# Rows of four q loads moved between DMA engines, in a kernel of sliding-window attention and spectral mixing on one core

## The chip, the core and the metric

The kernel runs on one core of a Trainium2 chip. The metric is the device time of one execution in microseconds (us). Before the change three runs gave 424.06, 424.40 and 424.67 us, median 424.4. The profiled execution took 424.43 us; its span, from the first to the last instruction, is 422.7 us.

## The reference, cut to what matters

```python
# q, k, v: (8, 8, 576, 64) float32; w_r, w_i: (64, 512, 512); w_ch: (512, 512)
scores = q @ k^T / 8, kept where 0 <= i - j < 64, softmax over j
x = (softmax @ v), the 8 heads side by side            # (8, 576, 512)
X = rfft(x, over the 576 positions)[:, :64]            # 64 modes
Yr = Xr w_r - Xi w_i ; Yi = Xr w_i + Xi w_r            # a 512x512 matrix pair for each mode
u = x + irfft(Y)
out = u + max(u @ w_ch, 0)
```

The 64 pairs of mode weights are 134 MB in float32 and are each used once. They are most of what the kernel reads: with q, k, v and `w_ch` it is 162.53 MB by the page's own account.

## The kernel before

The work goes in three stages. In the first (to about 142 us) eight batches of attention run, each with its rows of q, k and v loaded as bfloat16 (the transfer casts), turned on TensorE and used in windows of 512 score columns; the transform to 64 modes follows each batch. In the second (to about 389 us) the 127 weight matrices that are used are multiplied one after the other as they arrive; between them TensorE does the channel product and the inverse transform of what is complete. In the third the last rows are finished and written out.

All large loads are issued by GpSimd (POOL) in one order, and pass through the core's 16 DMA engines. `load` (line 117) loads one batch of q, k or v into a tile of 128 partitions with two runs of 2,304 bytes each; `load_w` (152) loads one mode's matrix, 4,096 bytes for each of 128 partitions, and `load_two` (157) loads two. A transfer over 128 partitions gives each DMA engine eight partitions: a q load is 16 packets of 2,304 bytes on each engine, a matrix 8 packets of 4,096.

The order in the first stage is written by hand. Unit 2, 5 and 8 of batch b's turning work frees the raw tile of k, v or q, and `refill` (422) then loads the same input of batch b + 2 and, if b > 0, one more early weight. So the requests go k, weight, v, weight, q, weight, batch after batch. The q loads of batches 4, 5, 6 and 7 are issued at 45.24, 58.27, 75.94 and 88.97 us. Eight DMA semaphores serve POOL's transfers in turn, so that each request also waits until the transfer eight before it has landed on all engines.

One load is uneven already (111 to 125): the q of batch 7. Its first 128 rows (the lower four heads) are split. 125 rows go as a transfer whose source is seen as 5 blocks of 25 rows with the block index outermost in the walk, so that 5 DMA engines carry 25 rows each and 11 carry none; the last 3 rows go by themselves; and a small transfer `aside` of 22 rows of 32 bytes in 11 blocks carries no data that is used. The code takes it that transfers on fewer than 16 engines get their engines in turn, and `aside` completes the turn: 5 and 11 engines. The upper 128 rows go evenly. As the 125 rows then lie in another order in the tile, the transposes of these rows use `back` (115, 262 to 264) instead of the identity: a permuted identity that two VectorE copies make from `ident_bf`.

`part` (258) turns six columns of a raw tile on TensorE into `pst`, and `evac` (55) copies them out.

Of the kernel before, what the change touches and what calls it, by code (L numbers as in the profile page):

```python
# [11 lines left out]
BF16 = mybir.dt.bfloat16  # L12
# [8 lines left out]
def view(ap, off, dims):  # L21

    return bass.AP(ap.tensor, ap.offset + off, [list(ap.ap[0])] + [list(d) for d in dims])
# [3 lines left out]
def kernel(  # L27
# [10 lines left out]
    nc = tc.nc  # L38
    B, H, S, D = q.shape
# [8 lines left out]
    RUN = S // 32  # L48
# [6 lines left out]
    def evac(o, i, on_act):  # L55

        if on_act:
            return nc.scalar.copy(out=o, in_=i)  # L58
        return nc.vector.tensor_copy(out=o, in_=i)  # L59
# [10 lines left out]
    ident_bf = consts.tile([128, 128], BF16, name="ident_bf")  # L70
# [19 lines left out]
    acons = p1.enter_context(tc.tile_pool(name="acons", bufs=1, side="right"))  # L90
# [12 lines left out]
    def raw_tile(which):  # L103
        return rawp.tile([128, 2, RUN * D], BF16, name="r" + which)

    def runs(b, which):
        return RAW[which][b].rearrange("(x g) (p c) d -> (g p) x (c d)", g=4, c=RUN)

    UNEVEN = (B - 1, "q")
    FEW, MORE = 5, 25
    LOT = FEW * MORE
    aside = acons.tile([2 * (16 - FEW), 16], BF16, name="aside")
    back = acons.tile([128, 128], BF16, name="back")

    def load(b, which):
        r = raw_tile(which)
        if (b, which) == UNEVEN:
            lower, upper = [RAW[which][b, x * H // 2:(x + 1) * H // 2].rearrange("g (p c) d -> (g p) (c d)", c=RUN)  # L120
                            for x in range(2)]
            nc.gpsimd.dma_start(out=r[:LOT, 0, :], in_=lower[:LOT].rearrange("(r a) c -> a r c", a=FEW))
            nc.gpsimd.dma_start(out=r[:, 1, :], in_=upper)
            nc.gpsimd.dma_start(out=r[LOT:, 0, :], in_=lower[LOT:])
            nc.gpsimd.dma_start(out=aside, in_=lower[:2 * (16 - FEW), 0:16].rearrange("(r a) c -> a r c", a=16 - FEW))
        else:
            nc.gpsimd.dma_start(out=r, in_=runs(b, which))
        raws[b, which] = r
# [65 lines left out]
    with tc.manual_schedule(engines=ALL_FOUR):  # L194
# [3 lines left out]
        with tc.tile_pool(name="tmpf", bufs=1, side="right") as tmp:  # L198
            mo = tmp.tile([128, NM], FP32, name="mo")
            to = tmp.tile([128, NT], FP32, name="to")  # L200
            nc.gpsimd.iota(mo, pattern=[[1, NM]], base=0, channel_multiplier=0,
                           allow_small_or_imprecise_dtypes=True)
            nc.gpsimd.iota(to, pattern=[[128, NT]], base=0, channel_multiplier=1,
                           allow_small_or_imprecise_dtypes=True)
            nc.gpsimd.memset(ident, 0.0)
            nc.gpsimd.affine_select(out=ident, in_=ident, compare_op=ALU.not_equal, fill=1.0,
                                    base=0, pattern=[[-1, 128]], channel_multiplier=1)
            load(0, "q")
            load(0, "v")
            for t0, t1 in ((0, 3), (3, NT)):  # L210
                n = t1 - t0
                mt = tmp.tile([128, 2, n * NM], FP32, name="mtf")
                nc.vector.tensor_tensor(out=view(mt, 0, [[NM, n], [1, NM]]), in0=view(mo, 0, [[0, n], [1, NM]]),
                                        in1=view(to, t0, [[1, n], [0, NM]]), op=ALU.mult)
                gen_trig(tmp, mt, n * NM, trigF[:, t0:t1, 0:NM], trigF[:, t0:t1, NM:2 * NM], "f")
                if t0 == 0:
                    nc.vector.tensor_copy(out=ident_bf, in_=ident)
        nc.scalar.activation(out=spark, in_=ident[:, 0:1], func=ACT_F.Exp)
        raws[0, "k"] = raw_tile("k")
        for c, engine in enumerate((nc.vector, nc.gpsimd, nc.vector)):  # L220
            cc = slice(6 * D * c, 6 * D * (c + 1))
            engine.tensor_copy(out=raws[0, "k"][:, :, cc], in_=k_first[:, :, cc])
        load(1, "k")
        for i in range(4):
            half = i % 2
# [24 lines left out]
    def transpose_units(b):  # L250

        rk, rq, rv = (raws.pop((b, which)) for which in "kqv")
        qT = qtp.tile([128, 4, S], BF16, name="qT")
        vT = vtp.tile([128, 4, S], BF16, name="vT")
        kT, vt = kTs[b % 2], vts[b % 2]
        qTs[b] = qT

        def part(src, dst, c0, on_act, uneven=False):
            def f():
                ps = ps_misc.tile([128, 6, 128], BF16, name="pst", tag="misc")  # L260
                if uneven and c0 == 0:
                    nc.vector.tensor_copy(out=back, in_=ident_bf)
                    nc.vector.tensor_copy(out=view(back, 0, [[1, FEW], [FEW, MORE]]),
                                          in_=view(ident_bf, 0, [[MORE, FEW], [1, MORE]]))
                for c in range(6):
                    for hh in range(2):
                        nc.tensor.transpose(out=ps[64 * hh:64 * hh + 64, c, :],  # L267
                                            in_=src[:, hh, (c0 + c) * D:(c0 + c + 1) * D],
                                            identity=back if uneven and hh == 0 else ident_bf)
                evac(view(dst, c0, [[S, 4], [RUN, 32], [1, 6]]),  # L270
                     view(ps, 0, [[32, 4], [1, 32], [128, 6]]), on_act)
            return f

        def vback(u):
            def f():
                ps = ps_misc.tile([128, 6, 128], BF16, name="psv", tag="misc")
                for i in range(6):
                    a, j = divmod(6 * u + i, 9)
                    if j == 4:
                        parts = [(0, 64, 2 * a, 512), (64, 64, 2 * a + 1, 0)]  # L280
                    else:
                        parts = [(0, 128, 2 * a + (j > 4), 128 * j - (j > 4) * S)]
                    for r0, n, g, t0 in parts:
                        nc.tensor.transpose(out=ps[r0:r0 + n, i, :],  # L284
                                            in_=vT[:, g, t0:t0 + n], identity=ident_bf)
                evac(view(vt, 6 * u * VW, [[18 * VW, 2], [VW, 6], [1, D]]),
                     view(ps, 0, [[D, 2], [128, 6], [1, D]]), u != 1)
                if u:
                    hs = slice(u - 1, u + 2, 2)
                    nc.vector.tensor_copy(out=vt[64:128, 1, hs, 1:9], in_=vt[64:128, 0, hs, 0:8])  # L290
                    nc.vector.tensor_copy(out=vt[0:64, 1, hs], in_=vt[0:64, 0, hs])
            return f

        return [part(rk, kT, 0, True), part(rk, kT, 6, False), part(rk, kT, 12, True),
                part(rv, vT, 0, False), part(rv, vT, 6, True), part(rv, vT, 12, False),
                *(part(rq, qT, 6 * i, i != 1, (b, "q") == UNEVEN) for i in range(3)),
                vback(0), vback(1), vback(2)]

    def head_of(n):
# [48 lines left out]
    def closes(w):  # L348

        return min(-(-8 * w // 9) * 9 or 9, 8 * w + 8)  # L350
# [92 lines left out]
    with tc.manual_schedule(engines=ALL_FOUR):  # L443
        first = transpose_units(0)
        for j in (0, 1, 2, 6, 7, 8):
            first[j]()
            refill(0, j)
            if j in (2, 8):
                warm_up(3)
        for half in range(2):  # L450
            pp = slice(64 * half, 64 * half + 64)
            nc.vector.tensor_copy(out=band2[pp], in_=band[pp, half, :])
        mask(0, 1)
        scores(0)
        for j in (3, 4, 5):
            first[j]()
            refill(0, j)
            warm_up(2)
        for vt in vts:
            nc.vector.memset(vt[:, 0, :, :, 64:66], 1.0)  # L460
        for j in (9, 10, 11):
            first[j]()
            refill(0, j)
        nc.vector.memset(pso, 1.0)
        nc.vector.tensor_copy(out=ident_r, in_=ident)
    with tc.manual_schedule(engines={E.PE, E.Pool}):
# [9 lines left out]
        def unit(b, j):  # L476
            if b not in units:
                units[b] = transpose_units(b)
            units[b][j]()
            refill(b, j)  # L480
            turned(b, j)

        for w in range(NWIN + 1):
# [5 lines left out]
            n = len(todo)  # L489
            if 0 < w < NWIN:  # L490
                scores(w)
            if w:
                cut = closes(w - 1)
# [12 lines left out]
            if w in (NWIN - 4, NWIN - 1):  # L506
                i = (B - 2) % 2 if w == NWIN - 4 else (B - 1) % 2
                spare(kTs[i])
                spare(qtp.tile([128, 4, S], BF16, name="qT"))
            if w in (NWIN - 4, NWIN):  # L510
                i = (B - 2) % 2 if w == NWIN - 4 else (B - 1) % 2
# [386 lines left out]
    for k, (f, delta, n, few) in enumerate(items):  # L898
        i = S_I + k * (T_I - 2 - S_I) // len(items)
# [25 lines left out]
    with tc.manual_schedule(engines=ALL_FOUR):  # L925
# [92 lines left out]
        for k in range(6):  # L1018
# [10 lines left out]
                              in_=view(psys[0], 0, [[2 * B, NC], [2, B], [1, 2]]))  # L1029
# [78 lines left out]
```

## Time and profile before

| what | value |
|---|---|
| time of the profiled execution, its span | 424.43 us, 422.7 us |
| median of three runs | 424.4 us |
| first stage, attention | 0 to 142 us |
| weights still to catch up with | 142 to 176 us |
| weights as they land | 176 to 389 us |
| last weight landed, on all engines | 389.20 us |
| from there to the end of the span | 33.5 us |
| transfers issued by POOL | 126 |

The page counts the busy time of each engine, shows the span in 40 slices, the DMA queues, and the chain of work that ended last. The chain is read from the last instruction back: each step is what released the one after it. The list of DMA issues gives each transfer's size and the time from issue to its last landing. Behind these views the trace holds two kinds of records that are used below: each DMA packet with its start and size, and for each of POOL's transfers the sixteen moments at which the sixteen engines report that their share has landed. A packet of four bytes is such a report, or takes the place of a row on an engine that has none. No record tells an engine's number.

### The profile page before, as it was taken

Reading aid. Unit: us, or ns where it says so; the run is one execution under the profiler, and the core shown is the slowest. Engines: PE = TensorE matmul, PEld = TensorE weight load, DVE = VectorE, ACT = ScalarE, POOL = GpSimd, SP = SyncE. Lnnn points to the kernel's source line nnn. Section 1 sums busy time; section 2 is a strip of 40 time slices with the busy share of each in tenths; the row PEclk is TensorE's granted clock in tenths of the full one; section 3 lists DMA queues with packets and bytes.
Section 4 is the critical chain, followed back from the end, with each engine's and each line's share of the span. In section 5 each row is a group of like instructions: output and inputs, shape, how many; then the busy total and the mean of one; then the engine's idle time right before and its main releaser. Section 6 shows DMA issues by size and latency. Waiting matters only on the chain.

```text
span 422.7 us, 11472 instructions
## 1 busy us (share of the span) xinstructions
PE 352.8 (83%) x5185; PEld 232.3 (55%) x5185; DVE 189.0 (45%) x361; ACT 159.9 (38%) x267; POOL 83.7 (20%) x149
## 2 busy tenths in 40 slices
PE   7899999999998779955758586757699998998994
PEld 3565666656654566744546455545466565554441
DVE  6576766775764100634342251211114344340895
ACT  5566866766765100122102110200023343330863
POOL 6231322232222230412112011210121212300000
PEclk9999999999999655978666656777569999999998
DMA  8999999999999999999999999999999999996598
GB/s 209 212 213 212 214 214 212 212 213 209 214 214 213 214 214 262 213 215 214 215 214 215 213 215 213 216 213 215 213 215 213 215 213 214 213 215 131 205 371 319
DMA packets 30288, 92.55 MB, mean 219 GB/s; under 512 B 2720, under 2 KB 2720, under 8 KB 30240
## 3 DMA queue, kind: packets, MB, share of 16 engines
q0 software_dynamic: 24992, 81.21, 96.3%
q1 hardware_dynamic: 5248, 10.62, 6.8%
q8 instruction: 40, 0.66, 0.6%
q14 instruction: 8, 0.07, 0.0%
HBM read 162.53 MB, written 9.44 MB: 407 GB/s over the span
## 4 chain that ended last, share of the span: by engine, by line
DMA 45%; PE 39%; DVE 7%; issue 2%; ACT 2%; DVEq 0%; POOLq 0%; ACTq 0%
DMA wms<-in_moe_w_i_dram 23%; DMA wms<-in_moe_w_r_dram 22%; PE psy L638 6%; PE pso L363 6%; PE pst L267 5%; PE psv L284 3%; PE psx L385 3%; PE pss L983 3%; DVE x_sb L371 2%; PE pss L976 2%; PE pss L320 2%; PE pss L339 2%; PE psz L779 2%; DVE vT L59 2%; PE psy L923 2%
## 5 line engine op out<-in xcount | busy, mean ns | idle before, releaser
L779 PE MATMUL psz<-wch,xT 128*128 128x512 f32 x144 | 61.2, 564 | 0.0
L773 DVE CAST xT<-pxt 128x1024 fp32r<-128x1024 bf16 x18 | 22.0, 1224 | 80.7 <-PE pxt L768 80.7
L782 ACT CAST Z<-psz 128x1024 fp32r<-128x1024 f32 x18 | 18.2, 1012 | 100.5 <-PE psz L779 100.5
L345 ACT ACTIVATE et<-pss 128x512 bf16<-128x512 f32 x72 | 39.2, 599 | 13.7 <-PE pss L339 13.7
L638 PE MATMUL psy<-XQ,wms 128*128 128x16 bf16 x624 | 25.0, 192 | 20.1 <-DMA wms<-in_moe_w_i_dram 12.3
L638 PE MATMUL psy<-XQ,wls 128*128 128x16 bf16 x560 | 21.9, 192 | 23.2 <-DMA wls<-in_moe_w_r_dram 14.4
L638 PEld LDWEIGHTS <-wms 128*128 128x128 bf16 x624 | 21.3, 102 | 32.3 <-DMA wms<-in_moe_w_i_dram 15.5
L779 PEld LDWEIGHTS psz<-wch,xT 128*128 128x128 f32 x144 | 34.9, 268 | 5.4
L638 PEld LDWEIGHTS <-wls 128*128 128x128 bf16 x560 | 19.6, 105 | 32.6 <-DMA wls<-in_moe_w_r_dram 17.2
L363 PE MATMUL pso<-vt,et 128*64 128x65 bf16 (+1 forms) x576 | 32.3, 203 | 3.5 <-DVE x_sb L371 1.6
L831 DVE TENSOR_TENSOR Z<-pse,Z 128x1024 fp32r<-128x1024 f32 x16 | 19.6, 1225 | 29.6 <-PE pse L820 29.6
L363 PEld LDWEIGHTS <-et 128*64 128x64 bf16 (+1 forms) x576 | 22.2, 108 | 14.2 <-issue 6.7
L371 DVE TENSOR_TENSOR x_sb<-pso,rcp 128x640 bf16<-128x640 f32 x32 | 26.3, 823 | 0.9
L638 PEld LDWEIGHTS <-wt 128*128 128x128 bf16 x560 | 18.4, 105 | 11.1 <-issue 4.2
L638 PE MATMUL psy<-XQ,wt 128*128 128x16 bf16 x560 | 20.5, 192 | 4.4 <-DMA wt<-in_moe_w_i_dram 1.7
L59 DVE COPY vT<-pst 128x768 bf16<-128x768 bf16 x16 | 15.3, 958 | 12.9 <-PE pst L267 11.3
L1001 ACT ACTIVATE pss<-pss 128x512 f32<-128x512 f32 x35 | 18.5, 581 | 4.7 <-PE pss L983 4.0
L59 DVE CAST YT<-psy 128x256 fp32r<-128x256 f32 x6 | 2.5, 423 | 38.6 <-PE psy L638 38.6
L923 PE MATMUL psy<-trigF,ident_bf 128*128 128x512 bf16 x46 | 18.4, 465 | 0.1
L284 PE MATMUL psv<-ident_bf,vT 128*128 128x128 bf16 (+1 forms) x160 | 15.7, 226 | 0.8 <-DVE vT L59 0.6
L320 PE MATMUL pss<-band,ident_bf 64*64 64x512 bf16 x120 | 16.3, 396 | 0.0
L58 ACT COPY vt<-psv 128x768 bf16<-128x768 bf16 x16 | 12.9, 808 | 8.5 <-PE psv L284 8.4
(198 smaller groups left out, 615.0 us busy)
## 6 DMA issues: line engine op xcount, KB each, us to landing
wt<-in_moe_w_i_dram POOLq DMA_DIRECT2D x19, 512.0 KB, 17.9
wt<-in_moe_w_r_dram POOLq DMA_DIRECT2D x16, 512.0 KB, 17.1
wls<-in_moe_w_r_dram POOLq DMA_DIRECT2D x8, 1024.0 KB, 21.7
wms<-in_moe_w_i_dram POOLq DMA_DIRECT2D x7, 1024.0 KB, 22.0
wms<-in_moe_w_r_dram POOLq DMA_DIRECT2D x7, 1024.0 KB, 21.2
wls<-in_moe_w_i_dram POOLq DMA_DIRECT2D x6, 1024.0 KB, 20.7
rv<-in_v_dram POOLq DMA_DIRECT2D x8, 576.0 KB, 13.0
rq<-in_q_dram POOLq DMA_DIRECT2D x7, 576.0 KB, 14.9
```

Of the source, the lines that this page charges most:

```text
L59: return nc.vector.tensor_copy(out=o, in_=i)
L267: nc.tensor.transpose(out=ps[64 * hh:64 * hh + 64, c, :], in_=src[:, hh, (c0 + c) * D:(c0 + c + 1) * D], identity=back if uneven and hh == ...
L284: nc.tensor.transpose(out=ps[r0:r0 + n, i, :], in_=vT[:, g, t0:t0 + n], identity=ident_bf)
L320: nc.tensor.matmul(out=pss[(2 * w + hh) % 3][64 * half:64 * half + 64, :], lhsT=ident_bf[pp, pp], rhs=view(band[pp], 128 * half, [[0, WIN ...
L345: nc.scalar.activation(out=et[:, hh, :], in_=pss[(2 * w + hh) % 3], func=ACT_F.Exp, scale=EX_SCALE)
L363: nc.tensor.matmul(out=pso[po, hh, block(b, i // 2) * VW:block(b, i // 2) * VW + D + 1], lhsT=et[pk, hh, col:col + 64], rhs=vt[pk, 1 - f % ...
L371: nc.vector.tensor_tensor(out=view(x_sb, b * NT * DM + g * D, [[4 * D, 2], [DM, NT], [1, D]]), in0=view(pso, 0, [[512, 2], [VW, NT], [1, D]]),
L638: nc.tensor.matmul(out=view(psy, off + 2 * B * e, [[1, 2 * B]]), lhsT=w[:, c, 128 * e:128 * e + 128], rhs=XQ[:, m // HM, c, :, 1 - im:3 - ...
L773: nc.vector.tensor_copy(out=o, in_=i)
L779: nc.tensor.matmul(out=psz[s][:, j, :], lhsT=xts[s % 2][0][:, j, 128 * c:128 * c + 128], rhs=wch[:, c, :], start=(c == 0), stop=(c == NC - 1))
L831: nc.vector.tensor_tensor(out=z, in0=ps, in1=z, op=ALU.add)
L923: nc.tensor.matmul(out=o, lhsT=ident_bf, rhs=view(trigF, 0, [[1, DM]]), start=True, stop=True)
```

## The change

Four q loads instead of one become uneven. Batch 4's q is now split as batch 7's was (5 engines with 25 rows each, then the upper rows, then the last 3), without the `aside`. Of the q of batches 5, 6 and 7 the first 34 rows go by a transfer whose source is seen as 17 blocks of 2 rows; 17 has no divisor from 2 to 16, and one engine carries all 34 rows. The other 94 of the lower rows follow the upper ones in a transfer of their own. Small transfers of 32-byte rows (`step_on`) move the turn: one engine ahead of the 34 rows for batches 5 and 6 (34 small rows on one engine), three engines ahead and three behind for batch 7 (two small rows on each). Counted that way from the turn's place at the start, the 5 engines are numbers 0 to 4, the single ones 6, 8 and 12, and the small ones 5, 7, 9 to 11 and 13 to 15.

Two permuted identities are made instead of one (for 5 blocks of 25 and for 17 blocks of 2), again by two copies each, and `part` takes the one that belongs to the batch. The transposes themselves keep their number and order, and so do all loads of k, v and weights. On POOL the four loads of q are 16 transfers instead of 7.

```diff
-    UNEVEN = (B - 1, "q")
-    FEW, MORE = 5, 25
-    LOT = FEW * MORE
-    aside = acons.tile([2 * (16 - FEW), 16], BF16, name="aside")
-    back = acons.tile([128, 128], BF16, name="back")
+    UNEVEN = {(4, "q"): (5, 25, RUN, 0, 0), (5, "q"): (17, 2, RUN, 1, 0), (6, "q"): (17, 2, RUN, 1, 0),
+              (7, "q"): (17, 2, RUN, 3, 3)}
...
+    aside = [acons.tile([34, 2, 16], BF16, name=f"aside{i}") for i in range(len(UNEVEN))]
+    forms = {lot[:2]: acons.tile([128, 128], BF16, name=f"back{lot[0]}") for lot in UNEVEN.values()}
...
+    def step_on(key, j, n):
+
+        n, src = (n if n > 1 else 17), k[0, :H // 2].rearrange("g (p c) d -> (g p) (c d)", c=RUN)
+        nc.gpsimd.dma_start(out=aside[list(UNEVEN).index(key)][:2 * n, j, :],
+                            in_=src[:2 * n, 0:16].rearrange("(r a) c -> a r c", a=n))
...
-        if (b, which) == UNEVEN:
+        if (b, which) in UNEVEN:
...
-            nc.gpsimd.dma_start(out=r[:LOT, 0, :], in_=lower[:LOT].rearrange("(r a) c -> a r c", a=FEW))
+            n, m, c, ahead, behind = UNEVEN[b, which]
+            if ahead:
+                step_on((b, which), 0, ahead)
+            cut = lower[:n * m].rearrange("(r a) c -> a r c", a=n)
+            nc.gpsimd.dma_start(out=r[:n * m, 0, :c * D], in_=cut[:, :, :c * D])
             nc.gpsimd.dma_start(out=r[:, 1, :], in_=upper)
-            nc.gpsimd.dma_start(out=r[LOT:, 0, :], in_=lower[LOT:])
-            nc.gpsimd.dma_start(out=aside, in_=lower[:2 * (16 - FEW), 0:16].rearrange("(r a) c -> a r c", a=16 - FEW))
+            if c < RUN:
+                nc.gpsimd.dma_start(out=r[:, 0, c * D:], in_=lower[:, c * D:])
+            nc.gpsimd.dma_start(out=r[n * m:, 0, :c * D], in_=lower[n * m:, :c * D])
+            if behind:
+                step_on((b, which), 1, behind)
...
-                                            identity=back if uneven and hh == 0 else ident_bf)
+                                            identity=back((b, which)) if hh == 0 and c0 + c < turned else ident_bf)
```

## The prediction

> **What bounds the kernel.** I read the slices first, then the queues and the chain, and then a table by stage.
>
> ```profile
> DMA  8999999999999999999999999999999999996598
> ...
> q0 software_dynamic: 24992, 81.21, 96.3%
> ...
> q8 instruction: 40, 0.66, 0.6%
> ...
> DMA 45%; PE 39%; DVE 7%; issue 2%; ACT 2%; DVEq 0%; POOLq 0%; ACTq 0%
> ```
>
> The DMA engines are busy from the first slice until slice 36, when the weights are in; POOL's queue is nearly all of it. Remember the 40 instruction packets.
>
> ```profile
> 142.00:176.00 34.00, 30.35 (x675) 24.88 (x675) 5.52 (x16) 2.31 (x5) 8.77 (x15) 0.58 1.08 229
> 176.00:389.00 213.00, 164.60 (x1880) 112.73 (x1879) 68.66 (x133) 47.24 (x68) 35.12 (x58) 0.79 1.05 212
> 389.00:395.00 6.00, 5.58 (x42) 3.25 (x42) 2.71 (x5) 2.80 (x6) 0.00 (x0) 1.00 0.01 3
> ```
>
> The column before the last is the DMA share: over 1 up to 389 us, then nothing, while TensorE (first pair) has room. The chain, in order of time, ends the stage so:
>
> ```profile
> 374.20 0.90 issue
> 375.12 14.08 DMA wms<-in_moe_w_i_dram
> 389.25 0.65 PE psy L638 x16
> 390.42 1.18 PE psy L988 x4
> ```
>
> The last weight's landing starts the tail, whose 33.5 us this change does not touch. A transfer has landed when the last of 16 engines reports, so **the time is set by the DMA engine that is done last**. The trace's sixteen reports of the last weight come 0, 0.31, 0.89, 4.35, 4.50, 4.91, 5.05, 5.35, 5.50, 5.68, 5.69, 5.70, 5.77, 5.81, 5.96 and 6.25 us after 382.95. Three engines are early; thirteen are late. Their mean is 4.47, so that perfect balance would be worth 1.8 us and no more.
>
> Why they differ: the 40 instruction packets of 16 KB take 0.89 to 0.98 us each, and their durations repeat with a period of eight. At each, one engine's reports fall back by as much. Eight engines thus lose about 4.7 us each by the end; eight have none. Five of these eight got 25 rows of batch 7's q, and were set back 4.2 to 4.4 us against the rest; three are left, the early ones.
>
> **Prices, from the records.** Along the weights of 108 to 133 us a 4,096-byte-by-8 share takes 2.460 us. A weight and a q-sized load in turn (70.22 to 101.67 us) take 5.243, so 16 rows take 2.78; their packets start 0.173 apart, which leaves 0.018 for a report. A row is 0.173 us.
>
> An engine without rows is not free. Between 126 transfers x 16 = 2,016 reports and the 2,314 four-byte packets in the trace there are 298 too many, and 298 = 11 engines x 25 + 13 x 1 + 5 x 2: in the uneven load each engine gets as many packets as the fullest one, padding of 4 bytes in place of rows. Price of one: on the earliest engine the uneven load and the next weight took 4.04 us; less 2.46, 8 upper rows (1.38) and 4 reports (0.07), 0.12 to 0.13 stay for 28 packets, 4.4 ns each. Followed packet by packet they start 6 ns apart. So 4.4 to 6; the bounds are nothing and the 22 ns that such a packet lasts.
>
> **The change, part by part.**
>
> *Batch 4 instead of batch 7 for the 25 rows:* the same work on the same queue, earlier. Nothing on the sum. Its missing `aside` is two packets an engine.
>
> *The 94 rows behind the 34.* Dealt to all engines from the first on, as the last 3 rows of the uneven load seem to be (see the rivals), they are six to an engine (the last four), where eight were: each engine saves 2 rows in each of three batches, 6 x 0.173 = 1.04 us.
>
> *The paddings.* Batches 5 and 6: 34 in the small transfer and 34 beside the single engine's rows, 68 each; batch 7: 2 + 34 + 2 = 38. In all 174, 0.77 to 1.04 us. POOL's transfers go from 126 to 135: 9 reports, 0.16. So an engine that carries no lot ends 1.04 less 0.93 to 1.20: **0.11 us earlier to 0.16 later**. What the uneven rows save, the padding eats. The small rows of 32 bytes start 5 ns apart in batch 7's `aside`, and count as padding.
>
> *The three single engines:* 34 + 6 rows for 8 in their own batch, 2 rows less in the other two: +28 rows, 4.84 us; 140 paddings 0.62 to 0.84; reports 0.16. Sum 5.62 to 5.84. The early engines at 0, 0.31 and 0.89 end at up to 6.51 to 6.73, while the last one today, at 6.25, ends at 6.14 to 6.41. So the last report moves by **0.26 to 0.48 us**; I take the middle, 0.37.
>
> *POOL and its queue.* Its issues cost it about 0.7 us each, which is free as long as requests come ahead of the engines.
>
> ```profile
> 88.97 0.70 POOL L122 DMA_DIRECT2D rq<-in_q_dram  x1 [2.24 <-PE pst L267]
> 89.68 0.57 POOL L123 DMA_DIRECT2D rq<-in_q_dram  x1
> 91.42 0.73 POOL L124 DMA_DIRECT2D rq<-in_q_dram  x1 [1.17 <-DMA rq<-in_q_dram]
> 93.89 0.56 POOL L125 DMA_DIRECT2D aside<-in_q_dram  x1 [1.73 <-DMA wt<-in_moe_w_r_dram]
> 96.92 0.55 POOL L154 DMA_DIRECT2D wt<-in_moe_w_i_dram  x1 [2.47 <-DMA rk<-in_k_dram]
> ```
>
> POOL, third and fourth lines, waits for DMAs: the transfer eight back must have landed everywhere. Small transfers use up these eight, and what queues behind is the next weight. After batch 7's q (now five) that weight waits for the weight that landed at 99.07, is asked for by about 100, and the earliest engine comes to it at 101.67 + 0.2 + 1.38 + 1.04 + 0.1, about 104.4. Nearly 4 us are left; if they were gone, each us lacking would be a us of idle on the engines that are ahead, which have it to spare. The q of batches 5 and 6 land up to 4 us later on the single engine (75.4 and 91.1 us before), some 10 us before their transposes.
>
> *Two more VectorE copies* for the second permutation:
>
> ```profile
> L262 DVE COPY back<-ident_bf x1: 195/195/195, 3.3 to 3.3; 128x128 bf16<-128x128 bf16 x1
> L263 DVE COPY back<-ident_bf x1: 508/508/508, 3.5 to 3.5; 128x125 bf16<-128x125 bf16 x1
> ```
>
> At most 0.70 us more at 3.5 us, and VectorE stands idle for 1.05 us before its cast at 6.02, where it waits for k. Hidden; without that, attention would be late by 0.4 us, behind a DMA backlog of over 10 us. The transposes stay.
>
> **Sum:** 424.43 + 0.37 = **424.8 us**, against a median of 424.4 (the profiled run stands at it).
>
> **Rivals.**
>
> *Padding costs nothing* (below 1 ns). Then the others gain 1.04 - 0.16 = 0.88 and end at 5.37, but the last single engine ends at 0.89 + 4.84 + 0.16 = 5.89, where 6.25 was: 0.36 us earlier, 424.1. For: some paddings may hide behind a row's end. Against: the 4.04 us above, and 25 rows (4.32) set engines back by only 4.21. Chance 0.11.
>
> *The single lots meet the wrong engines* (the slower side). No record carries an engine's number. What the trace shows: of the five loaded engines three were set back 4.38 us and two 4.21, so the 3 last rows fell on three of these five and did not move on to others. That fits lots that start at the first engine and a rest that is dealt out from there. That the three early ones are numbers 6, 8 and 12 is not shown; only the count fits: numbers 0 to 4 and these are eight, as many as have no instruction packets. If one lot falls on an engine that ends at 4.9 to 6.25 today, 5.7 us come on top: the last report 4.4 to 5.7 us later, **428.8 to 430.1**. It decides as soon as a single engine is over 0.9 us behind the earliest. Chance 0.13.
>
> *The 94 rows do not spread.* Were they dealt to two engines, 47 each (8.1 us), a pair would gain 39 rows in its batch and lose 16 in the other two, 4.0 us with 1 us of padding; engines at 5.7 would end at 10.7: about 429. The 3-row transfer speaks for spreading from the first engine on, but three rows are few. Chance 0.05. The Trainium skill, "DMA: Bandwidth & Descriptors", section "Why a DMA increments its semaphore by 16 and not by 1", has the rule behind this: the number of engines is the largest up to 16 that divides the slowest dimension, which for 94 is 2; it names as an exception that GpSimd's direct copies can use 16 with the rows rounded up, which gives the six above. Where the three rows fell agrees with the exception.
>
> *Padding or small rows cost more.* At 22 ns 174 of them are 3.8 us and the end moves by 3.0, 427.4; at 9 ns by 0.9. For: nothing shows 34 in a row on fifteen engines. Chance 0.05.
>
> *The end is not the DMA's:* other work hides the shift. TensorE waits 0.35 us for the last weight, so up to that a gain shows and a loss fully does. Within 0.2% either way. Chance 0.03.
>
> The same page, section "Anatomy of one DMA — SWDGE (gpsimd) path", fits 2.0 us of fixed cost to each transfer; nine more would by that be 18 us, 442. The 4.04 us for five transfers here speak against it, as they overlap in the queue.
>
> **Numbers.** Forecast 0.63, the rivals 0.11, 0.13, 0.05, 0.05 and 0.03. The predicted time is the forecast's. The range takes in the forecast, the free padding and the dear one up to 14 ns (174 x 0.014 + 0.16 - 1.04 = 1.6 us): 423.8 to 426.0, with the two rivals on wrong engines left out. About 0.2% (0.85 us) is what a measurement of this kernel can tell from no change. Faster by more than that 0.06 (free padding with a gain that I don't see), within 0.70, slower 0.24 (0.13 + 0.05 + 0.04 dear padding, 0.02 from the forecast's edge).
>
> **What would show it.** Right: the reports of the last weight within about 2.4 us instead of 6.25, none early; its landing at 389.5 us; about 5,060 four-byte packets in the trace (135 x 16 reports and 288 + 1,022 + 1,022 + 564 paddings); DMA share over 1 up to there. Wrong engines: one to three reports some 5 us behind all others from batch 5, 6 or 7 on. Free padding: the shares after batch 7 a full us ahead. Wrong altogether: gaps in the DMA engines after the q loads, or a wait on q in attention.

## The result: slower by 1.3%

The changed kernel takes 429.81 us (median of 4 runs, 429.70 to 429.95) against 424.31 for the kernel before on the same chip: ratio 1.0129, 95% interval 1.0112 to 1.0147. I had said 424.8 with a range of 423.8 to 426.0. The profiled execution took 429.70 us, with a span of 427.9.

### The profile after

The page first: slices, POOL's queue, the instruction queue, and the chain by engine.

```profile
DMA  8999999999999999999999999999999999994598
...
q0 software_dynamic: 27792, 81.22, 95.7%
...
q8 instruction: 40, 0.66, 0.6%
...
PE 43%; DMA 42%; DVE 7%; ACT 3%; issue 3%; POOL 1%; DVEq 0%; POOLq 0%; ACTq 0%
```

The bytes of POOL's queue are the same to 0.01 MB, in 2,800 more packets: 2,598 paddings, 144 reports and 58 of the small rows of 32 bytes. This queue has 5,056 four-byte packets, exactly 135 x 16 reports and the 2,896 paddings of the prediction. The digits of the slices tell nothing; the difference is in who is busy. The same stages as a table, first after, then before (busy time of each engine, clock, DMA share, GB/s):

```profile
95.00:117.00 22.00, 21.74 (x481) 14.60 (x484) 14.88 (x27) 16.22 (x29) 6.59 (x12) 1.00 1.05 196
...
142.00:176.00 34.00, 27.51 (x631) 22.97 (x636) 4.07 (x7) 2.19 (x5) 7.71 (x13) 0.56 1.08 229
...
345.00:394.00 49.00, 45.40 (x477) 27.83 (x483) 18.83 (x20) 16.07 (x21) 7.93 (x15) 1.00 0.97 193
394.00:400.00 6.00, 5.49 (x41) 3.08 (x41) 2.49 (x5) 2.59 (x6) 0.00 (x0) 1.00 0.01 3
```

```profile
95.00:117.00 22.00, 21.79 (x482) 14.57 (x477) 14.67 (x28) 15.96 (x28) 4.80 (x9) 1.00 1.08 211
...
340.00:389.00 49.00, 44.95 (x467) 26.89 (x465) 17.77 (x20) 15.45 (x20) 7.97 (x15) 1.00 1.02 204
```

The transfers end about 5 us later, and in the two stretches shown less is moved, 196 and 193 GB/s where it was 211 and 204. The chain at the end, after:

```profile
379.74 0.94 issue
380.70 13.70 DMA wms<-in_moe_w_i_dram
394.45 0.65 PE psy L663 x16
395.62 1.19 PE psy L1013 x4
```

It has the same form as before. The last weight lands at 394.40 instead of 389.20, 5.20 us later: this is the 5.2 us that the span has grown. Its sixteen reports come 0, 0.04, 0.09, 0.13, 0.19, 0.23, 0.34, 0.54, 1.81, 1.99, 2.22, 2.26, 2.32, 2.37, **5.36 and 5.68** us after 388.72. Fourteen engines are through by 391.1. Two are late.

Where the two come from can be followed from report list to report list. At batch 5's single lot one engine goes from 1.0 us behind the first to 6.67; at batch 6's one from 0.15 to 5.81; at batch 7's one from 2.2 to 7.8. Up to the end of the stream the first then falls back by about another 1.1 us four times and the third three times. Each time one of the 16 KB instruction packets runs, for the first always the sixth of a round of eight (at 100.8, 158.7, 259.7 and 371.2 us), for the third always the second (124.9, 195.1 and 316.9 us). The second lot's engine never falls back. So **two of the three single lots hit engines with instruction packets.** At the end the first is the one at 5.36 us, the third the one at 5.68.

### The profile page after: what moved, and what is told of

Its sections match the earlier page's. It is cut to its first block, busy times and chain, and to the rows that moved or that the text cites. A ratio compares the mean times of both kernels' runs of the same rounds, so it can differ in the third digit from the quotient of the medians.

```text
span 427.9 us, 11457 instructions
## 1 busy us (share of the span) xinstructions
PE 354.2 (83%) x5156; PEld 235.0 (55%) x5185; DVE 189.2 (44%) x363; ACT 160.0 (37%) x267; POOL 90.2 (21%) x158
## 4 chain that ended last, share of the span: by engine, by line
PE 43%; DMA 42%; DVE 7%; ACT 3%; issue 3%; POOL 1%; DVEq 0%; POOLq 0%; ACTq 0%
DMA wls<-in_moe_w_r_dram 21%; DMA wls<-in_moe_w_i_dram 14%; PE pso L388 6%; PE pst L292 5%; PE psy L663 5%; DMA wms<-in_moe_w_r_dram 3%; DMA wms<-in_moe_w_i_dram 3%; PE psv L309 3%; DVE x_sb L396 3%; PE psx L410 3%; PE pss L1008 2%; PE pss L1001 2%; PE pss L345 2%; PE psf L845 2%; PE pss L364 2%
## 5 line engine op out<-in xcount | busy, mean ns | idle before, releaser
L804 PE MATMUL psz<-wch,xT 128*128 128x512 f32 x144 | 63.9, 586 | 0.0
L804 PEld LDWEIGHTS psz<-wch,xT 128*128 128x128 f32 x144 | 36.4, 279 | 5.8
L793 PE MATMUL pxt<-ident_bf,x_sb 128*128 128x128 bf16 x144 | 15.9, 279 | 0.0
```

The source lines that it names most:

```text
L804: nc.tensor.matmul(out=psz[s][:, j, :], lhsT=xts[s % 2][0][:, j, 128 * c:128 * c + 128], rhs=wch[:, c, :], start=(c == 0), stop=(c == NC - 1))
```

## The experiments

The theory after the result: the turn's numbers 6 and 12, unlike 8, belong to engines that have instruction packets. The rival: the nine additional transfers fill POOL's eight, so that requests come late and DMA engines stand idle, whichever of them carries a lot. The timeline of POOL after batch 7's q speaks for looking at it:

```profile
94.03 0.96 POOL L147 DMA_DIRECT2D rq<-in_q_dram  x1
94.72 0.84 POOL L148 DMA_DIRECT2D rq<-in_q_dram  x1
97.15 0.55 POOL L151 DMA_DIRECT2D rq<-in_q_dram  x1 [1.59 <-DMA wt<-in_moe_w_r_dram]
99.92 0.56 POOL L135 DMA_DIRECT2D aside<-in_k_dram  x1 [2.22 <-DMA rk<-in_k_dram]
103.51 0.55 POOL L182 DMA_DIRECT2D wt<-in_moe_w_i_dram  x1 [3.02 <-DMA wt<-in_moe_w_r_dram]
```

The next weight was asked for at 103.51, after the weight eight back had landed at 103.22 on its last engine, the late one of batch 5. The first engine had reported batch 7's q at 103.08 and that weight only at 108.31, 5.2 us later for 2.46 us of packets. There were idle engines, then. Were they the cause?

In the edits below `UNEVEN` replaces that of the changed kernel, whose two lines are shown once; where an edit is to the kernel before, the text says so, and "..." stands for lines left out.

**One single lot alone, number 8.**

```diff
-    UNEVEN = {(4, "q"): (5, 25, RUN, 0, 0), (5, "q"): (17, 2, RUN, 1, 0), (6, "q"): (17, 2, RUN, 1, 0),
-              (7, "q"): (17, 2, RUN, 3, 3)}
+    UNEVEN = {(4, "q"): (5, 25, RUN, 0, 0), (6, "q"): (17, 2, RUN, 3, 7)}
```

> Of the three single lots only batch 6's is left, at the turn's number 8 as in the change; batches 5 and 7 load their q evenly, and small transfers of two rows on each engine carry the turn over 5 to 7 and 9 to 15. Theory (engines: 8 is an early one): others save 2 rows (0.35 us) and get 38 paddings (0.2 us) and reports, the lot ends at 5.7 us at most, before the last of today: 424.0 to 424.5. Rival (the queue: small transfers in POOL's eight leave engines without work whatever engine has the lot): 425 or more.

424.24 us against 424.42; ratio 0.9994, interval 0.9982 to 1.0006. No change, as the theory has it.

**One single lot alone, number 6.**

```diff
+    UNEVEN = {(4, "q"): (5, 25, RUN, 0, 0), (5, "q"): (17, 2, RUN, 1, 9)}
```

> Of the three single lots only batch 5's is left, at the turn's number 6 as in the change. Theory (engines: 6 has instruction packets): the last weight lands about 5 us later for this one engine alone, 428.7 to 430, as much as the whole change. Rival (the queue, or the three lots together): 424 to 425.5, since the queue has four transfers instead of nine in addition.

429.35 us; ratio 1.0109, interval 1.0083 to 1.0136: one lot on this engine costs nearly what the whole change does. Both kernels issue 129 transfers, so the number of requests does not tell them apart. The ends of the two chains, number 8 first, then number 6:

```profile
375.24 13.80 DMA wms<-in_moe_w_i_dram
389.09 0.65 PE psy L662 x16
```

```profile
380.23 13.75 DMA wms<-in_moe_w_i_dram
394.03 0.65 PE psy L662 x16
```

With number 6, fifteen engines have reported the last weight within 2.74 us of the first, and one comes at 4.93. The table of stages of that kernel separates cause and consequence:

```profile
95.00:117.00 22.00, 21.68 (x475) 14.29 (x475) 14.64 (x26) 15.07 (x27) 3.82 (x8) 1.00 1.08 213
345.00:394.00 49.00, 45.54 (x477) 27.93 (x483) 18.82 (x20) 16.23 (x21) 7.93 (x15) 1.00 0.94 186
```

The gap at 95 to 117 us is not there (1.08, 213 GB/s), and the time is. The loss of rate near the end is there with one lot alone. One request shows how it comes about, first in this kernel, then in the one before:

```profile
348.27 0.53 POOL L181 DMA_DIRECT2D wls<-in_moe_w_r_dram  x1 [6.42 <-PE psy L662]
```

```profile
341.95 0.53 POOL L154 DMA_DIRECT2D wls<-in_moe_w_r_dram  x1 [6.42 <-PE psy L638]
```

POOL waits for TensorE to free the tile, and TensorE takes up a weight only when its last engine has reported. In the kernel before, the request comes 4.2 us ahead of the first engine's report of the weight before it (346.13). Here it comes 0.7 us behind that report (347.61), and the first engine reports the new weight only at 353.11, 5.5 us later for 2.46 us of packets. The rival falls: idle engines follow from a late one. That the lot here is batch 5's and the harmless one above batch 6's is not the reason either: the kernels below with lots on numbers 7, 8 and 15 have lots in batch 5 too and are no slower.

**The price of padding.** The kernel before, and sixteen small transfers more.

```diff
...
+        if (b, which) in PADS:          # v of batch 2; k, v, q of batches 3 to 7
...
+            nc.gpsimd.dma_start(out=smalls[PADS.index((b, which))],
+                                in_=src[:34, 0:16].rearrange("(r a) c -> a r c", a=17))
```

> The kernel before with sixteen small transfers (34 rows of 32 bytes on one engine each, once round the turn), so that each engine gets 510 four-byte paddings, 34 small rows and 16 reports and nothing else changes. Theory (4.4 to 6 ns a padding, 0.018 us a report): 2.2 to 3.1 us and 0.3, some 0.2 for the small rows: 427.0 to 428.0. Rival (padding is free): 424.6. Rival (22 ns, as long as a packet lasts): 435 or more.

427.40 us; ratio 1.0064, interval 1.0045 to 1.0083. The last weight lands at 392.06, 2.86 us later; less 16 reports at 0.018, and divided by the 544 small packets of each engine (510 paddings and 34 rows of 32 bytes, which are counted alike), that is **4.7 ns a padding**. The stage of these transfers, this kernel first:

```profile
25.00:110.00 85.00, 82.48 (x1708) 54.18 (x1711) 58.38 (x107) 59.75 (x105) 32.93 (x47) 1.00 1.12 205
```

```profile
25.00:110.00 85.00, 82.50 (x1715) 54.03 (x1711) 57.79 (x106) 59.62 (x106) 22.40 (x37) 1.00 1.09 213
```

The DMA engines show more busy time and move 8 GB/s less: busy with packets that carry nothing.

**Which numbers are early? A first probe, which failed.**

```diff
+    UNEVEN = {key: (17, 1, RUN, 0, 0) for key in [(2, "v")] + [(b, w) for b in range(3, 8) for w in "kvq"]}
```

> Sixteen loads (v of batch 2, then k, v and q of batches 3 to 7) each send their first 17 rows by a transfer for one engine, the other 111 to all; nothing moves the turn, so that the sixteen single lots should go once round all engines, the first on the turn's number 0. Each lot sets one engine back by 17 - 1 rows, 2.8 us; from which offset it starts tells which engine it is. Theory (engines): numbers 0 to 4 and 8 are engines without instruction packets, 6 and 12 have them, two more without are among 5, 7, 9 to 11 and 13 to 15. Rival (the turn isn't what the code counts, or it differs from run to run): lots that hit one engine twice and another never, or 6 and 12 without instruction packets. As each engine gets one lot, the end should move little by the lots themselves; 32 more transfers and 272 paddings cost 1.8 to 2.2 us, and idle DMA engines some more: 426 to 430.

428.31 us in one run, but no single lots: 17 rows in 17 blocks of one row are a plain run of rows, and went to nine engines, eight with two rows and one with one (the paddings, 15 for it and one for the 111 rows, are 16 for each load, 256 in all, as counted in the trace). The rule of the Trainium skill's "DMA: Bandwidth & Descriptors", section "Why a DMA increments its semaphore by 16 and not by 1", that some of GpSimd's direct copies use 16 engines with the rows rounded up, would give these nine; the trace agrees, with these 256 paddings.

**A second probe.** The kernel before, with sixteen transfers of 34 rows of 512 bytes, two to a block.

```diff
...
+            n, j = divmod(PADS.index((b, which)) % 6, 2)
+            nc.gpsimd.dma_start(out=smalls[34 * n:34 * n + 34, j, :],
+                                in_=src[:34, 0:256].rearrange("(r a) c -> a r c", a=17))
```

> The first probe failed: with one row to a block its 17 rows went to nine engines. This one is the kernel before with sixteen further transfers of 34 rows of 512 bytes (data that nothing uses) with 2 rows to a block, one engine each and once round the turn, ahead of the loads of v of batch 2 and of k, v and q of batches 3 to 7. Each sets its engine back by some 1.3 to 1.7 us, and the sixteen reports tell which offset it had. Theory (the turn counts as the code has it): each engine is hit once; numbers 0 to 4 and 8 have no instruction packets, 6 and 12 have, and two more among 5, 7, 9, 10, 11, 13, 14 and 15 have none. Rival (the turn moves otherwise): an engine hit twice. Time: as the transfers hit all engines alike, 1.5 us and what the paddings cost (2.7 us): 428 to 430.

428.75 us in one run. One of the sixteen lots left ahead of all loads, at 1.56 us; the numbers here go by the order in which POOL issued the lots. Each lot moves one report by 1.2 us. Number 8's lot meets the engine that is first of all; number 7's one at 0.16, where no engine that had had an instruction packet was; number 15's the one that has become first by then. Numbers 5, 6 and 12 meet engines at 1.33, 1.07 and about 1.7 us, of which 6's had fallen back just before, by the sixth instruction packet. The durations of these packets begin at the same place of the round as in the changed kernel (935, 974, 974 ns here), where number 6's engine was the sixth as well. With the five that the prediction found, the engines without are 0 to 4, **7, 8 and 15**.

**The change on these three.**

```diff
+    UNEVEN = {(4, "q"): (5, 25, RUN, 0, 0), (5, "q"): (17, 2, RUN, 2, 0), (6, "q"): (17, 2, RUN, 0, 0),
+              (7, "q"): (17, 2, RUN, 6, 0)}
```

> The change with its three single lots on the turn's numbers 7, 8 and 15, the three that the second probe shows without instruction packets, instead of 6, 8 and 12; small transfers of two rows each carry the turn over 5 and 6 and over 9 to 14. Theory (the prediction's sum with the right engines): no engine lags; all others save 1.04 us and pay 106 paddings at 5.2 ns and 7 reports, 0.68 us, and the single ones end at 5.65 us where 6.25 was the last: 0.2 to 0.4 us under the kernel before, 423.9 to 424.2; the sixteen reports of the last weight within about 2 us. Rival (single lots cost something else besides, whichever engine has them): 425 or more.

424.12 us against 424.50; ratio 0.9991, interval 0.9982 to 0.9999. The last weight lands at 388.82, 0.38 us earlier, and the sixteen reports lie within 1.99 us instead of 6.25. This kernel has seven transfers more than the one before and three single lots, and loses nothing by them: what the change lost was lost by which engines its lots met.

**The same rows with fewer paddings.**

```diff
+    UNEVEN = {(4, "q"): (5, 25, RUN, 0, 0), (5, "q"): (2, 34, RUN, 2, 0), (6, "q"): (17, 2, RUN, 6, 0)}
```

> As the run before, but numbers 7 and 8 get their 34 rows each by one transfer of 2 blocks in batch 5, number 15 gets 34 in batch 6, and batch 7 is even: the same rows move with 72 paddings instead of 106 and 2 transfers less. Theory: 1.04 us saved less 0.37 and 0.09: 0.5 to 0.6 us under the kernel before, 423.7 to 423.9. Rival (what is late at the end is not the engines with most rows and instruction packets): as the run before or no change, 424.0 to 424.4.

423.80 us; ratio 0.9985, interval 0.9976 to 0.9994, landing at 388.68. The median is 0.15% under that of the kernel before. It is 0.32 us under that of the run just above, with ranges that overlap (423.67 to 424.31 here, 423.79 to 424.33 there), so that the order of these two is likely and not certain. The ends of the two chains, three single lots first, then this one:

```profile
375.03 13.79 DMA wms<-in_moe_w_i_dram
388.86 0.65 PE psy L663 x16
```

```profile
374.81 13.87 DMA wms<-in_moe_w_i_dram
388.73 0.65 PE psy L662 x16
```

**Batch 4 for batch 7 alone.**

```diff
+    UNEVEN = {(4, "q"): (5, 25, RUN, 0, 11)}
```

> Only the first part of the change: batch 4's q uneven as batch 7's was, with the 11 small ones behind it, and batches 5 to 7 even. Theory: nothing, 424.2 to 424.5. Rival (uneven early, the spread of the landings costs something through POOL's eight): over 424.8.

424.34 us; ratio 0.9998, interval 0.9989 to 1.0007. The move costs nothing.

## Why the prediction was wrong

- **The bound was right.** The last engine's report of the last weight sets the time: in every kernel here TensorE takes up the last weight 0.04 to 0.05 us after it, and the tail is the same, 33.4 to 33.5 us.
- **The step that failed is "The three single engines".** It put the 34 rows on the engines at 0, 0.31 and 0.89 us, that is, took the turn's numbers 6, 8 and 12 for the three early ones. No record told that; I rested it on a count (0 to 4 and these three make eight, and eight engines have no instruction packets). Eight is right, the numbers are not: 7, 8 and 15 are early, 6 and 12 are not. Any three of the eleven numbers left would have passed that count. The sum of 5.62 to 5.84 us for a lot was sound; two of the lots put it on engines that were 1.0 and 2.2 us behind the first and had packets still to come.
- **The rival had it,** with a chance of 0.13: one lot on a wrong engine, 4.4 to 5.7 us, 428.8 to 430.1. Measured: 5.20 us later, 429.81. Without a record, three of eleven numbers could be early, and the single lots meeting them all should not have been the likeliest case by five to one. That two lots went wrong and not one adds only 0.46 us to the run with number 6 alone: they are side by side, and the later one counts. In the change's trace number 6's engine reports the last weight at 394.08, where it came at 393.99 alone, and number 12's at 394.40.
- **The other terms hold.** 94 rows go to all sixteen engines: the 5,056 four-byte packets come out only so. Padding is 4.7 ns, between 4.4 and 6. With the right engines, 106 paddings at 4.7 ns (0.50) and 7 reports (0.13) against 1.04 us saved give 0.41 us; 0.38 was measured. That they agree this closely is partly luck, as the executions of that kernel range from 423.79 to 424.33. So the whole balance is worth 0.1%, and a lot on a wrong engine costs ten times that.
- **The queue** was taken for harmless with nearly 4 us in hand. These were used up: the weight after batch 7's q was asked for at 103.51 instead of about 100, as the landing it waits for had itself been set back by the late engine, which my estimate had left out. It cost the engines that were ahead about 2.7 us, and the end nothing: the two late engines had no gap there, as their reports of the small transfer before and of this weight are only 2.2 to 2.3 us apart.
- **Two readings were off,** and neither enters the sum. The mean of the sixteen reports before is 4.48 and not 4.47. And an engine falls back by about 1.1 us at an instruction packet (from 1.30 to 2.40 us behind the first at the packet of 69.96 us in the trace before), more than the 0.89 to 0.98 that the packet takes: some 5.5 us by the end and not 4.7.
- **VectorE's copies** were hidden, as said:

```profile
L127 DVE COPY back<-ident_bf x2: 187/188/189, 3.5 to 3.6; 128x128 bf16<-128x128 bf16 x2
L128 DVE COPY back<-ident_bf x2: 406/458/510, 3.7 to 4.0; 128x125 bf16<-128x125 bf16 x1, 128x34 bf16<-128x34 bf16 x1
```

All four are done by 4.5 us, ahead of the cast that waits for k until 6 us.

What stays open: why these eight engines have the instruction packets. Why a packet of 0.9 us costs 1.1 stays open too. That number 12 costs as much alone as number 6 was not run; it is read from the change's own trace.

## What to carry to other kernels

Where transfers bound a kernel and land on all engines together, look at the sixteen reports of one transfer and not at the busy share: the share was 0.94 or more wherever these kernels loaded weights and were looked at, the late ones too. Before load is moved to an engine, find out by a probe which one the transfer meets; a small lot on each number in turn answers that in one run. Load that is put aside for one engine is paid for by all others in padding, so that one transfer for two engines brings fewer paddings than two for one each.

## What the runs showed of the hardware

- A transfer for fewer than sixteen engines gives each of the others as many four-byte packets as the fullest one has rows: with the reports this makes 5,056 four-byte packets in POOL's queue for the change (the prediction's count), 4,000 for the three right lots and 2,908 for number 8 alone, and the traces have exactly these. One costs 4.7 ns of an engine, against 173 ns for a row of 2,304 bytes.
- The instruction packets go round eight engines, five to each in all these runs, but start at another one from run to run: their durations begin with 893, 893, 949 ns in the profile before and with 935, 975, 974 after, in the same cycle of eight. As far as the lots tell, the eight are the same in every run: number 6's engine has the packets in all three runs with a lot on it, number 8's in none.
- One engine that reports 5 us and more behind the others slows the other fifteen too, by way of requests that wait for landings: 186 GB/s instead of 204 in the last 49 us of the weights, with number 6 alone.
